# Float64 weights rebuilt with one VectorE instruction less, and a small add moved from VectorE to ScalarE, in an attention and expert kernel

## The chip, the cores and the metric

The kernel runs on one core of a Trainium2 chip. The metric is the device time of one execution in microseconds (us). The five engines are called by the profile's names: PE is TensorE (the matmuls; PEld its weight loads), DVE is VectorE, ACT is ScalarE, POOL is GpSimd, and SP issues DMAs.

## The reference

Three networks follow each other. Attention (4 batches, 8 heads, 512 local and 32 global tokens, head size 64) has a softmax whose sum gets 1e-9 added:

```python
def sm(s):
    s = s - np.max(s, axis=-1, keepdims=True)
    e = np.exp(s)
    return e / (np.sum(e, axis=-1, keepdims=True) + 1e-09)
```

Local tokens see 32 neighbours on either side and the global tokens; global tokens see all. Then a gated two-layer network follows, and a mixture of experts which sends each token to one of eight:

```python
xk = mu_k * x + (1.0 - mu_k) * x_prev
xr = mu_r * x + (1.0 - mu_r) * x_prev
k = np.maximum(xk @ w_k, 0.0)
v = k * k @ w_v
r = 1.0 / (1.0 + np.exp(-(xr @ w_r)))
return (r * v)
...
h = np.maximum(x[b, s] @ w1[e], 0.0)
out[b, s] = p[e] * (h @ w2[e])
```

The weights `w_k`, `w_r` and `w_v` of the middle network are multiplied by a float64 scalar when they are drawn, so they arrive as float64.

## The kernel before

`phase1` does the attention and the middle network, `Experts` the rest. `phase1` is a set of generators that a planner (`Sched`, lines 41 to 80) interleaves: each `yield op("D",.34)` names the engine of the instructions that follow and the duration which the planner assumes for them, with places in buffers that they need and free. The planner runs when the kernel is built. Its order is then sorted once more by the compiler's own model, and every engine works through its list in that fixed order.

`Attn` works on 16 units (a batch and a pair of heads); a unit has four items of 128 local tokens and one global item. `item` (line 195): PE makes the scores of two heads (L207); DVE adds the mask and takes the row's extreme (L213, two instructions); ACT takes the exponential with the sum beside it (L216, two); DVE adds 1e-9 to the two sums (L218, 128x2) and takes the reciprocal (L219); POOL multiplies (L222, two); PE transposes (L228); ACT and DVE copy the result out of PSUM; PE multiplies with the values (L236); ACT writes the result to `xT` (L240, L241). The probabilities lie in four buffers `pl`.

`Mix.weight` (line 386) brings one of 20 pieces of a float64 weight matrix (8 of `w_k`, 4 of `w_r`, 8 of `w_v`) into two float32 parts, a piece being 128x512 numbers. The high word of a float64 has an exponent field of 11 bits, of which the upper eight lie where a float32 has its exponent. The steps: ACT takes the absolute value of the high word, read as float32 (L403); DVE raises it to at least `LEAST` (L405), masks it and shifts it left by three (L407), puts in the sign and the upper exponent bit of the high word (L409) and three bits of the low word (L411); ACT rounds to the first part (L413); POOL subtracts to get the second (L415).

`Mix.mix` (line 430) blends each token with the one before it (POOL L441, DVE L444, ACT L446, POOL L448 into `xs`), and `Mix.run` multiplies (psk, psr, psv); these matmuls fill PE between the items of attention. When the last attention unit is done, `late` (line 726) frees the buffers of attention and loads the first expert weights into the tiles `st` (SP), which ACT (L778) and DVE (L781) split into two parts.

Of the kernel before, what the change touches and what calls it, by code (L numbers as in the profile page):

```python
# [10 lines left out]
F32=mybir.dt.float32; F32R=mybir.dt.float32r; BF=mybir.dt.bfloat16; I32=mybir.dt.int32  # L11
AF=mybir.ActivationFunctionType; ALU=mybir.AluOpType; X=mybir.AxisListType.X
# [1 line left out]
P=128; D=512; F=1024; E=8; SG=32; SL=512; S=544; NB=4; T=2176; HD=64; NK=9; NCH=17  # L14
NEG=-1e9
FRESH=-1.08674975e-07
LEAST=float(np.array(0x38000000,np.int32).view(np.float32))

def mm3(nc,out,wh,wl,xh,xl,first,last,order=None):

# [18 lines left out]
def op(e,d,need=(),free=(),when=None): return e,d,need,free,when  # L39
def wait(f): return "",0.0,(),(),f  # L40
# [42 lines left out]
class Attn:  # L83
# [111 lines left out]
    def item(s,u,i):  # L195


        nc=s.nc; b,pr=divmod(u,4); kw,qT=s.T[u]["k"],s.T[u]["q"]
        tag,n=("cm",3) if u<4 and i%2 else ("s",2)
        ks=slice(32*(i==0),224-32*(i==3)); w=1 if i in (1,2) else .87  # L200
        parts=s.parts(u)
        yield op("P",(.25+.13*len(parts) if len(parts)>1 else .8)*w,(tag,tag,"p"))
        S_=[s.ps.tile([P,512],F32,tag=tag,name="s_",bufs=n)[:,ks] for h in range(2)]
        for m,(x,y) in enumerate(parts):
            for h in range(2):
                r=slice(h*HD,(h+1)*HD)
                nc.tensor.matmul(S_[h],qT[r,x,i*P:(i+1)*P],kw[r,y,i,ks],start=m==0,stop=m==len(parts)-1)  # L207
        s.sdone[u]+=1
        p=s.pt_.pop(0)
        mx=s.sb.tile([P,8],F32,tag="mx",name="mx",bufs=5)  # L210
        yield op("D",.64*w,(),(tag,tag))
        for h in range(2):
            nc.vector.tensor_tensor_reduce(out=p[:,h,ks],in0=S_[h],in1=s.mask[:,ks],scale=-0.125,scalar=3e38,op0=ALU.add,op1=ALU.min,accum_out=mx[:,h:h+1])  # L213
        yield op("A",.93*w)
        for h in range(2):
            nc.scalar.activation(p[:,h,ks],p[:,h,ks],AF.Exp,bias=mx[:,h:h+1],scale=-1.0,accum_out=mx[:,4+h:5+h])  # L216
        yield op("D",.28)
        nc.vector.tensor_scalar(out=mx[:,4:6],in0=mx[:,4:6],scalar1=1e-9,scalar2=None,op0=ALU.add)  # L218
        nc.vector.reciprocal(mx[:,6:8],mx[:,4:6])  # L219
        yield op("G",.87*w)  # L220
        for h in range(2):
            nc.gpsimd.tensor_scalar(out=p[:,h,ks],in0=p[:,h,ks],scalar1=mx[:,6+h:7+h],scalar2=0.0,op0=ALU.mult,op1=ALU.add)  # L222
        yield op("P",.43,("pt","ph"),("p",),when=lambda: not s.early(u) or u in s.V)
        pt=s.ps.tile([P,2,2,P],F32,tag="pt",name="ptp",bufs=2)
        for c in range(2):

            for h in range(2):
                nc.tensor.transpose(pt[:,c,h],p[:,h,c*96:c*96+P],s.ident)  # L228
        s.pt_.append(p)
        P_=s.weights(u)  # L230
        yield from s.split(u,EV[i],P_,pt.rearrange("p c h q -> p c (h q)"),"pt",(.48,.61))
        yield op("P",.65 if len(parts)>1 else .87,("av",),("ph",),when=lambda: u in s.V)
        o=s.ps.tile([P,512],F32,tag="av",name="av",bufs=1)[:,:256]
        for c in range(2):
            for m,(x,y) in enumerate(parts):
                nc.tensor.matmul(o,s.v(u,x,i,c),P_[y][:,c],start=c==m==0,stop=c==1 and m==len(parts)-1)  # L236
        s.vdone[u]+=1
        yield op("A",.33,(),("av",))
        x=s.xT[b]; c0=1+SG+i*P
        nc.scalar.activation(x[0:64,pr,c0:c0+P],o[0:64,0:P],AF.Copy)  # L240
        nc.scalar.activation(x[64:128,pr,c0:c0+P],o[64:128,P:2*P],AF.Copy)  # L241
        yield wait(None)
        s.odone[u]+=1
# [3 lines left out]
    def v(s,u,w,i,c): return s.V[u][0][:,i,c] if s.early(u) else s.V[u][i//2][:,w,i%2,c]  # L247
# [83 lines left out]
class Mix:  # L331
# [54 lines left out]
    def weight(s,k,i):  # L386


        nc=s.nc; place="raw"+"v"*(k=="wv")
        yield op("Q",1.5,(place,))  # L390
        raws=s.raws[k=="wv"]; raw=raws.pop(0); raws.append(raw)
        v=lambda a: a[:,:,i*P:(i+1)*P] if k=="wk" else a[:,i:i+1]
        src=s.src[k].bitcast(I32).rearrange("(c p) (f t) -> p c f t",p=P,t=2)
        c=4 if k=="wk" else 1
        raw=raw.rearrange("p (c f t) -> p c f t",c=c,t=2); lo,hi=raw[:,:,:,0],raw[:,:,:,1]
        nc.sync.dma_start(raw.rearrange("p c f t -> p c (f t)"),v(src).rearrange("p c f t -> p c (f t)"))

        yield op("A",.52,("r",),when=lambda: k!="wv" or (s.may(S) and s.conv["wk"]==8 and s.conv["wr"]==4))
        if "wvh" not in s.W and k=="wv":
            for q,t in zip("hl",s.wplace()): s.W["wv"+q]=t.rearrange("p (c f) -> p c f",c=8)  # L400
        h,l=[v(s.W[k+x]) for x in "hl"]
        m=s.temp("w").rearrange("p (c f) -> p c f",c=c); a=m.bitcast(I32)
        nc.scalar.activation(m,hi.bitcast(F32),AF.Abs)  # L403
        yield op("D",.34)
        nc.vector.tensor_scalar(out=m,in0=m,scalar1=LEAST,scalar2=None,op0=ALU.max)  # L405
        yield op("D",.34)
        nc.vector.tensor_scalar(out=a,in0=a,scalar1=0x07FFFFFF,scalar2=3,op0=ALU.bitwise_and,op1=ALU.logical_shift_left)  # L407
        yield op("D",.6)
        nc.vector.scalar_tensor_tensor(out=a,in0=hi,scalar=-0x40000000,in1=a,op0=ALU.bitwise_and,op1=ALU.bitwise_or)  # L409
        yield op("D",.6,(),(place,))  # L410
        nc.vector.scalar_tensor_tensor(out=a,in0=lo,scalar=29,in1=a,op0=ALU.logical_shift_right,op1=ALU.bitwise_or)  # L411
        yield op("A",.52)
        nc.scalar.activation(h,m,AF.Copy)  # L413
        yield op("G",1.23,(),("r",))
        nc.gpsimd.tensor_sub(l,m,h.bitcast(F32))  # L415
        yield wait(None)
        s.conv[k]+=1
# [639 lines left out]
```

## Time and profile before

| what | us |
|---|---|
| median of 3 runs | 781.51 |
| lowest and highest run | 778.05, 782.53 |
| the profiled execution, its own time | 781.29 |
| its span in the trace | 779.6 |
| busy in the span: PE, DVE | 734.9, 509.7 |
| busy in the span: ACT, POOL | 396.5, 347.6 |

The span is what the profiler saw from the first to the last instruction; the time of the same execution is 1.7 us longer. Busy time is the time in which an engine had at least one instruction under way. An average over the span mixes stages: attention with the middle network runs to about 520 us, the experts after it.

### The profile page before, as it was taken

What the parts mean: (1) busy time and instruction counts of PE and PEld (TensorE: products, weight loads), DVE (VectorE), ACT (ScalarE), POOL (GpSimd) and SP (SyncE); (2) the same over time, 40 slices, a digit from 0 to 9 for tenths busy, and PEclk for the clock granted to TensorE, in tenths of its full rate; (3) what the DMA queues carried; (4) which work ended last, traced back from release to release, by engine and by line L of the source; (5) the groups of instructions that cost most, each with busy time, mean ns of one, the idle gap of its engine ahead of it and who ended that gap; (6) DMA issues with size and microseconds to landing.
All of it is one profiled execution on the core that took longest, in us unless ns stands there. A gap on an engine that the chain in (4) does not pass through costs nothing. (4 is left out here: it accounts for less than half of the span.)

```text
span 779.6 us, 14122 instructions
## 1 busy us (share of the span) xinstructions
PE 734.9 (94%) x4782; PEld 620.7 (80%) x4782; DVE 509.7 (65%) x1483; ACT 396.5 (51%) x985; POOL 347.6 (45%) x473
## 2 busy tenths in 40 slices
PE   6888888999999999999999899997999999999996
PEld 3655686888888888888888789775787999989884
DVE  6798878868487695696664875666764643617261
ACT  4796666665374664664663524233762622416151
POOL 6576756743537335545343342015553332514231
PEclk9998798999999999999999999999999999999998
DMA  6684123211211211212000500135875351705330
GB/s 156 156 226 126 58 76 106 57 51 36 65 31 27 64 40 37 65 32 78 12 13 28 175 32 12 57 107 215 284 266 209 122 178 39 271 30 182 123 98 17
DMA packets 93478, 77.04 MB, mean 99 GB/s; under 512 B 70462, under 2 KB 74558, under 8 KB 93378
## 3 DMA queue, kind: packets, MB, share of 16 engines
q1 hardware_dynamic: 89618, 64.27, 27.6%
q0 software_dynamic: 3760, 11.54, 4.1%
q8 instruction: 50, 0.82, 0.4%
q14 instruction: 50, 0.41, 0.2%
HBM read 66.87 MB, written 9.70 MB: 98 GB/s over the span
## 5 line engine op out<-in xcount | busy, mean ns | idle before, releaser
L222 POOL TENSOR_SCALAR pl<-pl,mx 128x192 f32<-128x192 f32 (+1 forms) x128 | 63.5, 508 | 86.8 <-DVE mx L219 41.6
L216 ACT ACTIVATE pl<-pl,mx 128x224 f32<-128x224 f32 (+1 forms) x128 | 58.8, 461 | 35.5 <-DVE mx L213 28.8
L21 PE MATMUL psk<-xs,slot0h 128*128 128x256 f32 x256 | 74.3, 296 | 0.8 <-ACT xs L446 0.8
L23 PE MATMUL psk<-xs,slot0h 128*128 128x256 f32 x256 | 73.6, 289 | 0.0
L24 PE MATMUL psk<-xs,slot0l 128*128 128x256 f32 x256 | 73.3, 288 | 0.0
L448 POOL TENSOR_TENSOR xs<-xm,xs 128x512 fp32r<-128x512 f32 (+1 forms) x36 | 46.3, 1298 | 40.9 <-ACT xs L446 40.9
L884 ACT ACTIVATE hh<-ph 128x256 fp32r<-128x256 f32 x56 | 21.6, 385 | 84.0 <-PE ph L24 82.8
L863 POOL DMA_INDIRECT xs<-y,idx x26 | 32.5, 1249 | 63.2 <-PE pt L870 39.2
L441 POOL TENSOR_SCALAR xm<-xT,mut 128x256 f32<-128x256 f32 (+7 forms) x96 | 42.7, 462 | 36.8 <-DVE xT L292 18.6
L932 POOL DMA_INDIRECT out_dram<-osb,idx x18 | 22.5, 1251 | 79.0 <-DVE osb L928 65.6
L21 PE MATMUL psv<-slot1h,kh 128*128 128x512 f32 x136 | 55.3, 407 | 0.0
L23 PE MATMUL psv<-slot1l,kh 128*128 128x512 f32 x136 | 54.3, 400 | 0.0
L24 PE MATMUL psv<-slot1h,kl 128*128 128x512 f32 x136 | 54.2, 398 | 0.0
L21 PEld LDWEIGHTS psk<-xs,slot0h 128*128 128x128 f32 x256 | 48.7, 193 | 1.8 <-ACT xs L446 0.9
L23 PEld LDWEIGHTS psk<-xs,slot0h 128*128 128x128 f32 x256 | 48.8, 191 | 1.2
L228 PE MATMUL ptp<-ident,pl 128*128 128x128 f32 x256 | 43.7, 291 | 6.1 <-DVE kw L119 1.3
L24 PEld LDWEIGHTS psk<-xs,slot0l 128*128 128x128 f32 x256 | 48.9, 191 | 0.6
L236 PE MATMUL av<-ph,v 128*128 128x256 f32 x192 | 45.0, 295 | 2.3 <-DVE xT L292 1.9
L885 DVE SCALAR_TENSOR_TENSOR hl<-ph,hh 128x256 fp32r<-128x256 f32 x56 | 23.7, 422 | 33.0 <-ACT hh L884 32.7
L444 DVE SCALAR_TENSOR_TENSOR xm<-xT,mut,xm 128x256 f32<-128x256 f32 (+7 forms) x96 | 41.3, 463 | 3.1 <-POOL xm L441 3.0
L119 DVE TENSOR_TENSOR plo<-ptp,ph 128x512 fp32r<-128x512 f32 x48 | 32.7, 684 | 14.9 <-ACT ph L117 14.7
L228 PEld LDWEIGHTS ptp<-ident,pl 128*128 128x128 f32 x256 | 30.4, 147 | 13.0 <-issue 3.1
(732 smaller groups left out, 2458.9 us busy)
## 6 DMA issues: line engine op xcount, KB each, us to landing
st<-in_moe_w_dram SPq DMA_DIRECT2D x42, 512.0 KB, 4.3
sw<-in_moe_w_dram SPq DMA_DIRECT2D x22, 512.0 KB, 4.3
y<-r SPq DMA_DIRECT2D x17, 256.0 KB, 2.1
qn<-in_q_l_dram SPq DMA_DIRECT2D x32, 128.0 KB, 2.9
kn<-in_k_l_dram SPq DMA_DIRECT2D x32, 128.0 KB, 3.0
earlyh<-in_moe_w_k_dram SPq DMA_DIRECT2D x8, 512.0 KB, 4.9
raw<-in_moe_w_v_dram SPq DMA_DIRECT2D x8, 512.0 KB, 3.8
vn<-in_v_l_dram SPq DMA_DIRECT2D x24, 96.0 KB, 2.1
```

The lines of the kernel that those rows point to most:

```text
L21: i=nc.tensor.matmul(out,wh,xh,start=first,stop=False)
L23: nc.tensor.matmul(out,wh,xl,start=False,stop=False)
L24: return nc.tensor.matmul(out,wl,xh,start=False,stop=last)
L119: nc.vector.tensor_sub(out[1],x,out[0].bitcast(F32))
L216: nc.scalar.activation(p[:,h,ks],p[:,h,ks],AF.Exp,bias=mx[:,h:h+1],scale=-1.0,accum_out=mx[:,4+h:5+h])
L222: nc.gpsimd.tensor_scalar(out=p[:,h,ks],in0=p[:,h,ks],scalar1=mx[:,6+h:7+h],scalar2=0.0,op0=ALU.mult,op1=ALU.add)
L228: nc.tensor.transpose(pt[:,c,h],p[:,h,c*96:c*96+P],s.ident)
L236: nc.tensor.matmul(o,s.v(u,x,i,c),P_[y][:,c],start=c==m==0,stop=c==1 and m==len(parts)-1)
L441: nc.gpsimd.tensor_scalar(out=x[:,u,o:o+k],in0=s.xT[b][:,c,q:q+k],scalar1=m[:,1,c:c+1],scalar2=0.0,op0=ALU.mult,op1=ALU.add)
L444: nc.vector.scalar_tensor_tensor(out=x[:,u,o:o+k],in0=s.xT[b][:,c,1+q:1+q+k],scalar=m[:,0,c:c+1],in1=x[:,u,o:o+k],op0=ALU.mult,op1=ALU.add)
L448: nc.gpsimd.tensor_sub(xl[:,cs,:n],x[:,:,:n],xh[:,cs,:n].bitcast(F32))
L863: s.nc.gpsimd.indirect_dma_start(out=s.xs[i][:,j,:],out_offset=None,in_=s.y,in_offset=IndirectOffsetOnAxis(ap=s.idx[:,ch:ch+1],axis=0))
```

## The change

The absolute value on ACT (L403) becomes a copy with a scale of 2 to the -112. That lowers the float32 exponent by 112, which is 896 in the 11-bit field; a magnitude that is too small becomes zero there, so the raising to `LEAST` on DVE is gone. The sign is kept through the scaling, so the mask has one bit more and the later step takes the sign alone from the high word. In `item` the addition of 1e-9 moves from DVE to ACT, as a copy with a bias on a 128x2 tile, in the same group as the exponentials; the planner's durations follow. Behind line 406 all numbers of the changed kernel are two lower: its L405 is the mask and shift that was L407, its L407 and L409 are the steps that were L409 and L411, its L411 is the rounding that was L413.

```diff
--- before.py
+++ after.py
@@ -14,7 +14,7 @@
 P=128; D=512; F=1024; E=8; SG=32; SL=512; S=544; NB=4; T=2176; HD=64; NK=9; NCH=17
 NEG=-1e9
 FRESH=-1.08674975e-07
-LEAST=float(np.array(0x38000000,np.int32).view(np.float32))
+REBIAS=2.0**-112
 
 def mm3(nc,out,wh,wl,xh,xl,first,last,order=None):
 
@@ -211,11 +211,11 @@
         yield op("D",.64*w,(),(tag,tag))
         for h in range(2):
             nc.vector.tensor_tensor_reduce(out=p[:,h,ks],in0=S_[h],in1=s.mask[:,ks],scale=-0.125,scalar=3e38,op0=ALU.add,op1=ALU.min,accum_out=mx[:,h:h+1])
-        yield op("A",.93*w)
+        yield op("A",.2+.93*w)
         for h in range(2):
             nc.scalar.activation(p[:,h,ks],p[:,h,ks],AF.Exp,bias=mx[:,h:h+1],scale=-1.0,accum_out=mx[:,4+h:5+h])
-        yield op("D",.28)
-        nc.vector.tensor_scalar(out=mx[:,4:6],in0=mx[:,4:6],scalar1=1e-9,scalar2=None,op0=ALU.add)
+        nc.scalar.activation(mx[:,4:6],mx[:,4:6],AF.Copy,bias=1e-9)
+        yield op("D",.15)
         nc.vector.reciprocal(mx[:,6:8],mx[:,4:6])
         yield op("G",.87*w)
         for h in range(2):
@@ -400,13 +400,11 @@
             for q,t in zip("hl",s.wplace()): s.W["wv"+q]=t.rearrange("p (c f) -> p c f",c=8)
         h,l=[v(s.W[k+x]) for x in "hl"]
         m=s.temp("w").rearrange("p (c f) -> p c f",c=c); a=m.bitcast(I32)
-        nc.scalar.activation(m,hi.bitcast(F32),AF.Abs)
+        nc.scalar.activation(m,hi.bitcast(F32),AF.Copy,scale=REBIAS)
         yield op("D",.34)
-        nc.vector.tensor_scalar(out=m,in0=m,scalar1=LEAST,scalar2=None,op0=ALU.max)
-        yield op("D",.34)
-        nc.vector.tensor_scalar(out=a,in0=a,scalar1=0x07FFFFFF,scalar2=3,op0=ALU.bitwise_and,op1=ALU.logical_shift_left)
+        nc.vector.tensor_scalar(out=a,in0=a,scalar1=0x0FFFFFFF,scalar2=3,op0=ALU.bitwise_and,op1=ALU.logical_shift_left)
         yield op("D",.6)
-        nc.vector.scalar_tensor_tensor(out=a,in0=hi,scalar=-0x40000000,in1=a,op0=ALU.bitwise_and,op1=ALU.bitwise_or)
+        nc.vector.scalar_tensor_tensor(out=a,in0=hi,scalar=-0x80000000,in1=a,op0=ALU.bitwise_and,op1=ALU.bitwise_or)
         yield op("D",.6,(),(place,))
         nc.vector.scalar_tensor_tensor(out=a,in0=lo,scalar=29,in1=a,op0=ALU.logical_shift_right,op1=ALU.bitwise_or)
         yield op("A",.52)
```

The planner's times are different, so the whole order of `phase1` is. Three places follow, each as built, before and then with the change.

The list of VectorE near its start, where the first pieces of `w_k` (`w`, `earlyh`) stand between the mask additions (`pl`, `mx`) of the first items. Before:

```order
L405 TENSOR_SCALAR w<-w 128x512
L407 TENSOR_SCALAR w<-w 128x512
L213 ISA pl_112,mx<-s__270,mask 128x192
L213 ISA mx 128x1
L409 SCALAR_TENSOR_TENSOR w<-earlyh,w 128x512
L405 TENSOR_SCALAR w<-w 128x512
L213 ISA pl_112,mx<-s__271,mask 128x192
L213 ISA mx 128x1
L411 SCALAR_TENSOR_TENSOR w<-earlyh,w 128x512
L407 TENSOR_SCALAR w<-w 128x512
L213 ISA pl_113,mx<-s__280,mask 128x224
L213 ISA mx 128x1
```

With the change:

```order
L405 TENSOR_SCALAR w<-w 128x512
L407 SCALAR_TENSOR_TENSOR w<-earlyh,w 128x512
L213 ISA pl_112,mx<-s__218,mask 128x192
L213 ISA mx 128x1
L409 SCALAR_TENSOR_TENSOR w<-earlyh,w 128x512
L405 TENSOR_SCALAR w<-w 128x512
L213 ISA pl_112,mx<-s__219,mask 128x192
L213 ISA mx 128x1
L213 ISA pl_113,mx<-s__225,mask 128x224
L213 ISA mx 128x1
L407 SCALAR_TENSOR_TENSOR w<-earlyh,w 128x512
L213 ISA pl_113,mx<-s__226,mask 128x224
```

The L405 of before is gone, and the steps of a piece stand closer together; no addition L218 is left on this engine.

The list of ScalarE over the same items (`slot0h` is the first part of `w_k`, rounded). Before:

```order
L216 ACTIVATE pl_112,mx<-pl_112,mx 128x192
L403 ACTIVATE w<-earlyh 128x512
L216 ACTIVATE pl_112,mx<-pl_112,mx 128x192
L413 ACTIVATE slot0h<-w 128x4x128
L216 ACTIVATE pl_113,mx<-pl_113,mx 128x224 x2
L216 ACTIVATE pl_114,mx<-pl_114,mx 128x224
L111 ACTIVATE earlyl<-ptq 128x4x128
L216 ACTIVATE pl_115,mx<-pl_115,mx 128x192
L413 ACTIVATE slot0h<-w 128x4x128
```

With the change:

```order
L216 ACTIVATE pl_112,mx<-pl_112,mx 128x192
L411 ACTIVATE slot0h<-w 128x4x128
L403 ACTIVATE w<-earlyh 128x512
L216 ACTIVATE pl_112,mx<-pl_112,mx 128x192
L216 ACTIVATE pl_113,mx<-pl_113,mx 128x224
L217 ACTIVATE mx<-mx 128x2
L216 ACTIVATE pl_113,mx<-pl_113,mx 128x224
L217 ACTIVATE mx<-mx 128x2
L411 ACTIVATE slot0h<-w 128x4x128
```

An addition L217 stands behind the exponentials of its item, here one row behind or with another item's exponential between. In the whole list there are 64, between one and four rows behind the second exponential of their item; the first 27 stand 2.15 rows behind it on the mean, so that 1.15 rows lie between.

The list of ScalarE where attention ends and the first expert weights come in (`og` is the last global item, `xs` the blended tokens, `st` the loaded weights, `slot2h` their first part). Before:

```order
L285 ACTIVATE og<-avg,mxg 64x128
L558 ACTIVATE lt<-psl 10x128
L446 ACTIVATE xs<-xm 128x512
L778 ACTIVATE slot2h<-st_5851 128x1024
L446 ACTIVATE xs<-xm 128x512
L603 ACTIVATE ex,sums<-L,nmx 128x8 x2
L778 ACTIVATE slot2h<-st_5852 128x1024
L778 ACTIVATE slot2h<-st_5853 128x1024
```

With the change:

```order
L285 ACTIVATE og<-avg,mxg 64x128
L556 ACTIVATE lt<-psl 10x128
L776 ACTIVATE slot2h<-st_5814 128x1024
L444 ACTIVATE xs<-xm 128x512
L601 ACTIVATE ex,sums<-L,nmx 128x8 x2
L444 ACTIVATE xs<-xm 128x512
L776 ACTIVATE slot2h<-st_5815 128x1024
L776 ACTIVATE slot2h<-st_5816 128x1024
```

Before, the first of the two blends L446 stands ahead of the first split L778; with the change both blends (L444 there) stand behind the first split (L776 there).

## Rows read from the trace of the kernel before

**Rows 1.** The page: busy totals of all engines, then VectorE (DVE) in 40 slices of 19.5 us.

```profile
PE 734.9 (94%) x4782; PEld 620.7 (80%) x4782; DVE 509.7 (65%) x1483; ACT 396.5 (51%) x985; POOL 347.6 (45%) x473
...
DVE  6798878868487695696664875666764643617261
```

**Rows 2.** Windows, all engines: start:end, length, busy us (instructions) each, PEclk, DMA share, GB/s.

```profile
14.00:145.00 131.00, 113.29 (x630) 85.06 (x630) 109.98 (x324) 91.99 (x271) 86.35 (x113) 0.90 0.44 118
145.00:380.00 235.00, 234.29 (x1768) 201.86 (x1767) 168.77 (x611) 134.41 (x395) 114.28 (x193) 1.00 0.18 46
...
430.00:442.00 12.00, 8.97 (x73) 8.07 (x73) 10.90 (x37) 7.16 (x15) 4.08 (x4) 0.86 0.49 175
```

**Rows 3.** Windows, all engines: two shorter stretches of the first stage.

```profile
14.00:20.00 6.00, 5.23 (x15) 2.25 (x14) 6.00 (x22) 3.81 (x14) 4.56 (x6) 1.00 0.44 61
44.00:68.00 24.00, 18.91 (x95) 12.42 (x95) 23.78 (x67) 19.68 (x57) 16.80 (x18) 0.93 0.81 220
```

**Rows 4.** Waits of TensorE (PE), 14 to 160 us: releaser, us in total, times, longest.

```profile
PE av L236 <- DVE xT L292: 1.4, 1, 1.4
PE ptp L228 <- DVE kw L119: 1.3, 1, 1.3
PE s__1065 L207 <- DVE mx L213: 1.3, 1, 1.3
```

**Rows 5.** Groups of VectorE instructions, 14 to 145 us: shape xcount | busy, mean ns | idle.

```profile
L405 DVE TENSOR_SCALAR w<-w 128x512 f32<-128x512 f32 x17 | 11.6, 681 | 0.4 <-ACT w L403 0.3
...
L407 DVE TENSOR_SCALAR w<-w 128x512 int32<-128x512 int32 x18 | 8.8, 488 | 0.1
L218 DVE TENSOR_SCALAR mx<-mx 128x2 f32<-128x2 f32 x27 | 8.7, 325 | 4.2 <-ACT pl L216 4.1
```

**Rows 6.** Windows of single VectorE lines: L405 in one stretch, then L218 in two.

```profile
44.00:68.00 24.00, 4.64 (x6) 0.93 0.81 220
...
14.00:20.00 6.00, 1.59 (x2) 1.00 0.44 61
44.00:68.00 24.00, 1.42 (x4) 0.93 0.81 220
```

**Rows 7.** Timeline of VectorE, then one row of GpSimd (POOL), 43 to 51 us: start, us.

```profile
43.52 0.41 DVE L405 TENSOR_SCALAR w<-w 128x512 f32<-128x512 f32 x1
43.85 0.68 DVE L411 SCALAR_TENSOR_TENSOR w<-earlyh,w 128x512 int32<-128x512 int32 x1
...
48.49 0.15 DVE L218 TENSOR_SCALAR mx<-mx 128x2 f32<-128x2 f32 x1
48.55 0.48 DVE L114 COPY ph<-ptg 128x320 f32<-128x320 f32 x1
...
49.88 1.16 DVE L405 TENSOR_SCALAR w<-w 128x512 f32<-128x512 f32 x1
...
49.44 1.31 POOL L415 TENSOR_TENSOR slot0l<-w,slot0h 128x512 fp32r<-128x512 f32 x1 [0.59 <-ACT slot0h L413]
```

**Rows 8.** Groups of ScalarE (ACT) instructions, whole run: shape xcount | busy, mean ns | idle.

```profile
L403 ACT ACTIVATE w<-earlyh 128x512 f32<-128x512 f32 x12 | 8.1, 672 | 3.6 <-DMA earlyh<-in_moe_w_k_dram 3.3 <-DMA earlyh<-in_moe_w_r_dram 0.3
...
L603 ACT ACTIVATE ex<-L,nmx 128x8 f32<-128x8 f32 x17 | 4.9, 291 | 1.4 <-DVE nmx L589 1.4
```

**Rows 9.** Timeline of ScalarE, then GpSimd, then TensorE, 434 to 438 us.

```profile
434.92 0.63 ACT L446 ACTIVATE xs<-xm 128x512 fp32r<-128x512 f32 x1 [0.41 <-DVE xm L444]
436.42 1.06 ACT L778 ACTIVATE slot2h<-st 128x1024 fp32r<-128x1024 f32 x1 [0.87 <-DMA st<-in_moe_w_dram]
437.38 0.61 ACT L446 ACTIVATE xs<-xm 128x512 fp32r<-128x512 f32 x1
...
435.63 1.27 POOL L448 TENSOR_TENSOR xs<-xm,xs 128x512 fp32r<-128x512 f32 x1 [0.92 <-ACT xs L446]
...
435.60 0.62 PE L21 MATMUL psk<-xs,slot0h 128*128 128x256 f32 x3 [0.81 <-ACT xs L446]
...
437.75 0.56 PE L23 MATMUL psk<-xs,slot0h 128*128 128x256 f32 x1
```

## The prediction

> **What bounds the kernel now.** I read the busy totals first, then the windows, then the waits of TensorE, and last single lines. The totals name TensorE: 734.9 us busy of a span of 779.6 [rows 1]. What a change on VectorE and ScalarE can give lies in TensorE's gaps and in its lower clock, so the question is where those are. The windows answer it [rows 2]. From 145 to 380 us TensorE is busy for 234.3 of 235 us at full clock: whatever VectorE saves there is hidden behind matmuls. From 14 to 145 us it is busy for only 113.3 of 131 us, and the granted clock is 0.90 on the mean. So 17.7 us are idle, and about 113.3 x 0.10 = 11.3 us more go to the lower of its two clock levels. That stage is where the change can pay. The slices show VectorE at its fullest in it [rows 1], and the shorter windows show two stretches where VectorE has no gap left: 6.00 of 6 us from 14 to 20, 23.8 of 24 us from 44 to 68, while ScalarE has over four us free in the second [rows 3]. There VectorE sets the pace. In the rest of the stage it is busy for 110.0 - 29.8 = 80.2 of 101 us, and TensorE waits for it only now and then: three waits that VectorE ended there make 4.0 us [rows 4].
>
> **The conversion of the weights.** Per piece one 128x512 instruction leaves VectorE, L405; 17 of the 20 lie in the stage, 11.6 us by their durations [rows 5]. What an absent one gives back has two ends. The next instruction starts 0.33 us after an undisturbed one (43.52 to 43.85), the least; the most is its whole duration, 0.68 us on the mean, which contains waits [rows 5, 7]. ScalarE's scaled copy takes the place of the absolute value on the same tile; I count no difference, between nothing and 0.1 us for each of 20 at 0.67 us [rows 8], and ScalarE has the room.
>
> **The addition of 1e-9.** 64 additions leave VectorE, 27 of them in the stage, 8.7 us by their durations [rows 5]. The ends again: the next instruction starts 0.06 us after an undisturbed one [rows 7], and the mean duration is 0.325. On ScalarE no such instruction exists in the trace. The nearest is the exponential of a 128x8 tile, 0.291 us [rows 8]; the bounds are nothing and twice that row, because the addition waits for the sum of its own engine. I take 0.29, the row itself: 27 x 0.29 = 7.8 us more, so ScalarE goes from 92.0 to 99.8 of 131 us [rows 2]. In the full stretch it has 19.7 of 24 us and gets four or five of them, 1.4 us. It stays below VectorE, so I count nothing on the path. The other 37 lie beside matmuls that leave TensorE no gap; were that cover gone, they would cost at most 37 x 0.29 = 10.7 us.
>
> **What of it lies on the path.** In the two full stretches are six L405 and six L218: 4.64 + 1.59 + 1.42 = 7.65 us by duration [rows 6], and 6 x 0.33 + 6 x 0.06 = 2.3 us by the distance of starts. Between them lie the waits. One is seen in the rows: L405 at 49.88 takes 1.16 us and ends shortly after a GpSimd instruction that ran from 49.44 for 1.31 us [rows 7]. When the instruction is gone, its wait is either gone too or passes to the next one on VectorE. The rows favour neither end, so I take the middle, 5.0 us. In the rest of the stage 6.9 + 5.7 = 12.6 us leave 80.2 us of work, 16%; applied to the 4.0 us of waits that gives 0.6 us. The clock I leave as it is: it is 1.00 where TensorE has no gap (145 to 380 us) and 0.93 in the full stretch with its 5.1 us of gaps [rows 2, 3], and no row says how many gaps must go before it holds. Its bounds are 0 and the 11.3 us above.
>
> The Trainium skill ("SBUF — State Buffer", section "SBUF: two separate sides") says that VectorE and GpSimd lock a shared pair of ports against each other for a whole instruction, and that a VectorE instruction with two SBUF inputs takes part as well. By that rule the two-input steps of the conversion, which stay, inherit the wait; the sum would then go by the lower end, 2.3 us instead of 5.0. The wait in rows 7 agrees with the lock.
>
> **Where attention ends.** The order is made anew, and at one place I can price it. Before, ScalarE's first blend L446 starts at 434.92, ahead of the first split L778, which had to wait for a DMA and starts at 436.42; the blend behind that split starts at 437.38 [rows 9]. With the change the first blend stands behind the split: 2.46 us later. GpSimd's second part follows 0.08 us after the blend and takes 1.27, so it would end at 437.38 + 0.63 + 0.08 + 1.27 = 439.36, and TensorE's matmul that started at 437.75 would start at about 439.4. I count +1.7 us, between 0 (the DMA comes sooner) and +2.5 (all of the delay). SP's loads are reordered too, expert weights excepted; I count nothing; a load that comes late would cost about as much as that DMA wait, 0.87 us [rows 9], and this stays in the range.
>
> **Sum.** -5.0 - 0.6 + 1.7 = -3.9 us against the profiled execution's 781.29 (span 779.6; the execution lies 0.2 us below the median 781.51): **777.4 us**. With the ends above the forecast's own range is 773.0 (-7.65 - 0.6) to 781.5 (-2.3 + 2.5).
>
> **The rivals.**
> *The wait passes on.* If the next VectorE instruction inherits each wait for GpSimd, the relief is 2.3 us, and outside the full stretches 11 x 0.33 + 21 x 0.06 = 4.9 us, 6% of 4.0, or 0.2. With +1.7 that is 780.5, no change that a measurement of this kernel can tell (that takes about 0.5%, 3.9 us). For it: the rows of the conversion stand closer together than before, on the same ports, and L407, which stays, has waits of its own (0.488 us on the mean [rows 5]). Against it: a later instruction often finds GpSimd idle, as GpSimd is busy for 86 of 131 us [rows 2].
>
> *A larger gain.* Gaps and the lower clock stand together in the rows, and matmuls at the lower clock make the items late. If half of the gaps (8.9 us) and half of the clock's loss (5.7 us) come back, the sum is -8.9 - 5.7 + 1.7 = -12.9, or 768.4. For it: VectorE is the busiest helper in the whole stage [rows 2]. Against it: outside the full stretches the rows name VectorE for only 4.0 us of TensorE's waits [rows 4].
>
> *Slower: the addition waits in ScalarE's list.* The 27 additions of the stage stand behind 1.15 other rows on the mean. At 0.67 us a row [rows 8], with ScalarE busy for 92 of 131 us, a row takes 0.67 / 0.70 = 0.96 us, so the reciprocal comes 1.1 us later. Four buffers `pl` are in turn, so a delay of 1.1 us for 27 items makes 27 / 4 x 1.1 = 7.4 us. With the small relief (2.3 + 0.2) and +1.7 this is 787.9. It decides, against the forecast's -3.9, from a delay of 3.9 x 4 / 27 = 0.58 us per item. For it: the order itself. Against it: before, the same addition stood in the list of an engine that was fuller still.
>
> **Chances.** Forecast 0.47, wait passes on 0.23, larger gain 0.13, slower 0.17. The limit for faster is 777.6: the forecast's range lies a little more below it than above, so 0.27 of it go to faster and 0.20 to the same; the larger gain goes to faster, and 0.02 of the passing wait. Of the slower rival 0.15 stay slower. That gives faster 0.42, same 0.43, slower 0.15. The range 770 to 786 leaves out the far halves of the outer two cases, about 0.17.
>
> **What would show it.** In the new profile: VectorE below 95 of 131 us in 14 to 145; no full stretch of 24 us there; 64 additions on ScalarE of about 0.3 us; the last item of unit 8 earlier by about 5 us; the first blend near the end of attention behind the first split and 1 to 2.5 us of new TensorE idle there. If VectorE's remaining conversion steps are longer than before (L407 was 0.488), the wait passed on. If GpSimd's multiplications wait longer for the reciprocal, the slower rival is right. The forecast is wrong if the stage to 145 us is not shorter although VectorE has gaps.

## The result: slower by 1.4%, and the profile after

| | median, us | lowest to highest, runs |
|---|---|---|
| before | 782.80 | 778.05 to 785.27, 6 |
| with the change | 793.47 | 791.35 to 795.40, 6 |

The ratio is 1.0139 with a 95% interval of 1.0106 to 1.0173. The forecast was 777.4 us, its range 770 to 786. The profiled execution of the changed kernel took 791.35 us, its span is 789.6.

The page of the changed kernel, busy totals and VectorE's slices (before: [rows 1]):

```profile
PE 739.8 (94%) x4782; PEld 624.1 (79%) x4782; DVE 492.2 (62%) x1399; ACT 408.1 (52%) x1049; POOL 347.7 (44%) x473
...
DVE  6588588667584686585674784567665553627261
```

VectorE has 84 instructions and 17.5 us less, ScalarE 64 instructions and 11.6 us more, as the change says. TensorE has the same 4782 matmuls, and they keep it busy for 4.9 us longer. The windows of the changed kernel (before: [rows 2, 3]):

```profile
14.00:145.00 131.00, 113.29 (x653) 85.76 (x654) 97.06 (x278) 96.70 (x294) 87.18 (x115) 0.92 0.44 118
145.00:380.00 235.00, 229.79 (x1663) 196.09 (x1661) 157.75 (x560) 132.95 (x406) 111.52 (x187) 0.99 0.18 45
14.00:20.00 6.00, 4.68 (x15) 2.60 (x15) 5.98 (x23) 4.68 (x17) 3.58 (x6) 1.00 0.43 60
44.00:68.00 24.00, 17.98 (x85) 11.88 (x85) 21.69 (x59) 21.66 (x69) 18.41 (x20) 0.87 0.79 227
```

The full stretch of 24 us is gone (21.69 in place of 23.78); that from 14 to 20 us is as full as before (5.98 of 6). VectorE is 12.9 us less busy in 14 to 145 us, and TensorE is busy for exactly as long there as before. The surprise is the second row: in 145 to 380 us, where TensorE had no gap, 5.2 us of 235 are idle now and the granted clock is 0.99.

To see where the 10 us came in, the two spans are cut at points where the same work is done: the last transpose of unit 4 (the lists hold the same numbers of psk, psr, psv, av and score matmuls ahead of it in both orders), that of unit 16 (the same), and the last matmul of psy, behind which only experts follow. The windows between these points, before:

```profile
0.00:96.73 96.73, 78.06 (x377) 54.15 (x377) 76.85 (x245) 65.97 (x197) 64.81 (x113) 0.91 0.55 145
96.73:432.29 335.56, 327.15 (x2420) 281.38 (x2420) 242.00 (x841) 192.70 (x558) 165.12 (x268) 0.98 0.18 47
432.29:516.82 84.53, 81.11 (x508) 69.11 (x509) 55.95 (x171) 33.05 (x65) 26.51 (x32) 0.98 0.24 85
516.82:779.60 262.78, 248.61 (x1478) 216.10 (x1478) 134.91 (x229) 104.76 (x166) 91.16 (x60) 0.98 0.44 152
```

and with the change:

```profile
0.00:96.21 96.21, 75.74 (x376) 53.78 (x376) 65.50 (x208) 68.11 (x212) 62.20 (x113) 0.93 0.55 146
96.21:439.60 343.39, 333.25 (x2420) 284.16 (x2419) 234.35 (x789) 202.18 (x607) 169.00 (x269) 0.98 0.18 46
439.60:527.12 87.52, 82.28 (x511) 69.88 (x511) 57.38 (x175) 33.17 (x65) 25.40 (x32) 0.96 0.23 82
527.12:789.60 262.48, 248.48 (x1478) 216.32 (x1478) 134.92 (x229) 104.69 (x166) 91.13 (x60) 0.99 0.45 152
```

The front gained 0.5 us, the middle (units 5 to 16) lost 7.8, the hand-over lost 3.0, the experts are as before. In the middle the 2420 matmuls (single records can be missing) keep TensorE busy for 6.1 us longer, and 1.7 us more are idle.

The groups of VectorE in 14 to 145 us with the change (before: [rows 5]), then the addition on ScalarE, whole run:

```profile
L405 DVE TENSOR_SCALAR w<-w 128x512 int32<-128x512 int32 x18 | 10.7, 593 | 4.4 <-ACT w L403 4.4
L407 DVE SCALAR_TENSOR_TENSOR w<-earlyh,w 128x512 int32<-128x512 int32 x11 | 10.7, 970 | 0.1
...
L219 DVE RECIPROCAL mx<-mx 128x2 f32<-128x2 f32 x24 | 3.8, 158 | 3.5 <-ACT mx L217 3.4
...
L217 ACT ACTIVATE mx<-mx 128x2 f32<-128x2 f32 x64 | 12.6, 198 | 0.9
```

Before, the mask and shift took 0.488 us on the mean [rows 5], and the step behind it is this group:

```profile
L409 DVE SCALAR_TENSOR_TENSOR w<-earlyh,w 128x512 int32<-128x512 int32 x11 | 7.7, 704 | 0.0
```

So the mask and shift went from 0.488 to 0.593 us, and the next step from 0.704 to 0.970: part of the waits did pass on to the steps that stay. Not every group got longer: the same next step on the pieces of `w_v` (8 of them, input `raw`) went from 1.124 to 0.987. The three steps that stay together are busy for 45.4 us in 14 to 145 us, 41.1 before, so about 4 of the 11.6 us of L405 came back in them. VectorE also waits 4.4 us for the scaled copy L403 now.

### The profile page after: what moved, and what is told of

It reads as the page before. It is cut to its first block, busy times and chain, and to the rows that moved or that the text cites. A ratio compares the mean times of both kernels' runs of the same rounds, so it can differ in the third digit from the quotient of the medians.

```text
span 789.6 us, 14015 instructions
## 1 busy us (share of the span) xinstructions
PE 739.8 (94%) x4782; PEld 624.1 (79%) x4782; DVE 492.2 (62%) x1399; ACT 408.1 (52%) x1049; POOL 347.7 (44%) x473
## 5 line engine op out<-in xcount | busy, mean ns | idle before, releaser
L21 PE MATMUL psk<-xs,slot0h 128*128 128x256 f32 x256 | 75.4, 301 | 3.5 <-ACT xs L444 3.5
L23 PE MATMUL psk<-xs,slot0h 128*128 128x256 f32 x256 | 75.0, 294 | 0.0
L446 POOL TENSOR_TENSOR xs<-xm,xs 128x512 fp32r<-128x512 f32 (+1 forms) x36 | 45.7, 1278 | 40.1 <-ACT xs L444 32.9
L23 PE MATMUL psv<-slot1l,kh 128*128 128x512 f32 x136 | 55.6, 409 | 2.9 <-POOL slot1l L413 2.9
L21 PEld LDWEIGHTS psk<-xs,slot0h 128*128 128x128 f32 x256 | 49.4, 196 | 5.0 <-ACT xs L444 4.0
L23 PEld LDWEIGHTS psk<-xs,slot0h 128*128 128x128 f32 x256 | 49.9, 195 | 1.1 <-issue 0.2
L228 PE MATMUL ptp<-ident,pl 128*128 128x128 f32 x256 | 45.4, 295 | 3.1 <-DVE g L385 0.8
```

Of the source, the lines that this page charges most:

```text
L21: i=nc.tensor.matmul(out,wh,xh,start=first,stop=False)
L23: nc.tensor.matmul(out,wh,xl,start=False,stop=False)
L446: nc.gpsimd.tensor_sub(xl[:,cs,:n],x[:,:,:n],xh[:,cs,:n].bitcast(F32))
```

## The experiments

Fifteen kernels ran, each beside the kernel before; each does the whole computation. In the kernels called pinned, a table of the instructions of each engine keeps the planner and the compiler's model from choosing the order of `phase1` (shortened; `ORDER` holds the table):

```diff
     sched.run()
+    keep_order(tc,ORDER)
     return m
...
+def keep_order(tc,text):
...
+    L={}
+    for i in tc.nc.cur_bb.bb.instructions: L.setdefault(str(i.engine).split(".")[-1],[]).append(i)
+    for e,o in tables.items():
+        for a,b in zip(o,o[1:]):
+            tc.add_manual_dep(L[e][b],L[e][a].name,mybir.DependencyInfo(mybir.DependencyClass.NoSync,mybir.DependencyReason.SCHED_ONLY))
```

### Instructions and order apart: four pinned kernels

**The change's instructions in the order of before** (ORDER is the order of before without L405, each addition directly behind its item's second exponential).

> The changed instructions in exactly the order of before on all five engines (TensorE, GpSimd and SP row for row; the removed rows gone, each addition directly behind the second exponential of its item on ScalarE). Theory A, the new order costs the time: 778 to 783 us, at most 0.5% from before, and a little faster if VectorE's relief reaches TensorE at all (my prediction's term was -5.6 us, that is 776). Theory B, the instructions cost it (the addition delays the reciprocal on ScalarE, the scaled copy is slower): 790 to 795 us, like the change.

Measured: 778.38 us, ratio 0.9929 (0.9904 to 0.9954).

**The instructions of before in the change's order** (the reverse: the absent instructions are put directly ahead of the steps that they stood ahead of).

> The instructions of before in the order of the change on TensorE, GpSimd and SP row for row; the clamp stands directly ahead of its mask and the addition directly ahead of its reciprocal on VectorE. Theory A: 790 to 800 us, as slow as the change or slower, since VectorE keeps its 84 instructions. Theory B: 778 to 784 us, like before.

Measured: 809.93 us, ratio 1.0332 (1.0307 to 1.0357). Theory A had the way right, but its range ended at 800 us.

**The weights' part alone, and the addition alone, in the order of before** (the first two kernels' edit, one half of the change's diff each).

> Only the weights' part (scaled copy, no clamp) in the order of before; the addition stays on VectorE. Theory A: 776 to 782 us, -0 to -5 us against before, as much as the relief of VectorE by 20 instructions in the first stage gives. Theory B with the copy as its cost: over 786 us; with the addition as its cost: like before.

Measured: 776.46 us, ratio 0.9914 (0.9888 to 0.9940).

> Only the addition moved to ScalarE, in the order of before; the clamp stays. Theory A: 779 to 784 us, within 0.5% of before (0.19 us each on ScalarE in the profile of the change, 27 in the first stage). Theory B with the addition as its cost: over 786 us.

Measured: 783.55 us, ratio 1.0006 (0.9983 to 1.0029).

What follows: the change's instructions are faster by 0.7%, and all of that is the weights' part; the moved addition gives nothing. The new order costs 2.1% under the new instructions (0.9929 to 1.0139) and 3.3% under the old ones, so it suits a lighter VectorE, as it was made for one, but it loses with both. The middle and the hand-over of the first of these kernels stand near those of before:

```profile
0.00:93.25 93.25, 75.86 (x376) 52.88 (x377) 69.09 (x211) 69.68 (x217) 62.91 (x113) 0.93 0.57 151
93.25:430.13 336.88, 327.73 (x2421) 281.53 (x2420) 231.72 (x791) 200.79 (x602) 165.50 (x269) 0.98 0.18 47
430.13:515.77 85.64, 82.55 (x508) 70.47 (x508) 55.45 (x171) 33.16 (x65) 26.53 (x32) 0.96 0.24 84
```

Against the changed kernel it is 6.5 us shorter in the middle and 1.9 us at the hand-over. These two profiled executions lie 10.5 us apart, the medians 15.1 us: the one is the slowest of its kernel's six, the other the fastest. The middle goes with the order: in the profiles of all five kernels with the order of before on TensorE (one of them joins six items, see below) it takes 335.6 to 336.9 us, in the changed kernel and the four that repair places of its order 343.4 to 345.4, and with the instructions of before in the changed order 348.9. The changed kernel's loss is its order.

### Three places of the new order, repaired one by one

**The hand-over.** In the changed kernel ScalarE's first split L776 waits for its weights, and the first blend L444 behind it (before: [rows 9]). TensorE's rows there, then ScalarE's:

```profile
443.81 0.37 PE L592 MATMUL psr<-ident,fe 128*1 128x128 f32 x1 [1.12 <-DVE fe L586]
445.95 1.01 PE L21 MATMUL psk<-xs,slot0h 128*128 128x256 f32 x3 [1.76 <-ACT xs L444]
447.84 0.37 PE L592 MATMUL psr<-ident,fe 128*1 128x128 f32 x1 [0.88 <-DVE fe L586]
...
444.32 1.06 ACT L776 ACTIVATE slot2h<-st 128x1024 fp32r<-128x1024 f32 x1 [3.30 <-DMA st<-in_moe_w_dram]
445.28 0.61 ACT L444 ACTIVATE xs<-xm 128x512 fp32r<-128x512 f32 x1
```

The repair, as lists of the engines and not as code:

```diff
 ScalarE
+L444 xs<-xm
 L776 slot2h<-st
-L444 xs<-xm
 VectorE
+L586 fe<-fe,base,fr
 L779 slot2l<-st,slot2h
-L586 fe<-fe,base,fr
```

> The changed kernel in its own order, with two pairs of instructions exchanged where attention ends: ScalarE's first blend L444 stands ahead of the first split L776 again, and VectorE's second step of fe (L586) ahead of the first L779. The changed kernel has 793.5 us. Theory A (the order at this place costs what the trace shows): from the transpose avt of the last unit to the second matmul psk on the new tokens it takes 439.60 to 447.86, 8.26 us, before 432.29 to 437.75, 5.46 us; the difference of 2.8 us comes back, 790.7 us, and TensorE's wait of 1.76 us for the blend is gone. Theory B (the loads of the expert weights set the end of this place, whichever engine waits for them first): the wait returns a few us later, 793.5 us as before the exchange.

Measured: 790.98 us, ratio 1.0143 (1.0088 to 1.0197). The place itself got shorter: from the last avt (438.58) to the second row of psk, L23 at 444.70, it takes 6.1 us in place of 8.3 (439.60 to 447.86). Not all of it came back: a gap of 2.15 us stands a step earlier now, where it was 1.12, because L586 is held beside a GpSimd instruction. TensorE, VectorE and GpSimd in the repaired kernel:

```profile
443.82 0.37 PE L592 MATMUL psr<-ident,fe 128*1 128x128 f32 x1 [2.15 <-DVE fe L586]
...
442.52 1.37 DVE L586 SCALAR_TENSOR_TENSOR fe<-fe,base,fr 128x1 f32<-128x1 f32 x2
...
442.49 1.26 POOL L446 TENSOR_TENSOR xs<-xm,xs 128x512 fp32r<-128x512 f32 x1 [0.92 <-ACT xs L444]
```

The 2.1 us at this place are below what six runs with this scatter (789.74 to 800.25 us) can show, so the gain of this repair stays unclear.

**Near 325 us.** VectorE, then GpSimd, then TensorE in the changed kernel:

```profile
325.63 1.17 DVE L581 SCALAR_TENSOR_TENSOR fr<-L,first 128x2 f32<-128x2 f32 x1
326.72 0.34 DVE L213 CUSTOM_DVE_ANT_0 pl<-s__4432,mask 128x192 f32<-128x192 f32 x1
...
324.29 2.49 POOL L192 TENSOR_TENSOR v<-vn,v 128x512 fp32r<-128x512 f32 x2
...
327.13 0.37 PE L207 MATMUL s__4472<-kw,qT 64*128 64x224 f32 x1 [1.58 <-DVE mx L213]
```

A 128x2 instruction lasts 1.17 us and ends at 326.80, GpSimd's at 326.78. The window behind it shows TensorE at the lower of its two levels throughout:

```profile
328.00:334.00 6.00, 6.00 (x26) 4.66 (x26) 3.39 (x19) 4.36 (x20) 3.84 (x6) 0.50 0.27 61
```

```diff
 VectorE
+L213 pl,mx<-s__4432,mask
+L213 pl,mx<-s__4433,mask
 L580 mx<-L
 L581 fr<-L,first
-L213 pl,mx<-s__4432,mask
 L582 m<-L,mx
-L213 pl,mx<-s__4433,mask
```

> The changed kernel in its own order, with five instructions of VectorE in another order near 325 us: the two mask additions L213 of the first item of unit 13 come ahead of L580, L581 and L582 of the router. In the changed kernel L581, a 128x2 instruction, lasts 1.17 us from 325.63 beside a GpSimd instruction with two SBUF inputs (324.29 for 2.49 us), the mask additions wait behind it, TensorE idles 1.58 us and then runs at half clock from 328 to about 335 us, 3.4 us lost. Theory A (the wait behind L581 starts it, and the clock follows the gap): the gap shrinks to about 0.5 us, the clock holds, 1.1 + 3.4 = 4.5 us come back, 789.0 us. Theory A, smaller: the gap shrinks but the clock falls all the same, 792.4 us. Theory B (the mask additions are held beside GpSimd just as L581 is): nothing comes back, 793.5 us, and L213 lasts over 1 us there.

Measured: 793.88 us, ratio 1.0139 (1.0097 to 1.0181). VectorE and TensorE there:

```profile
332.50 0.36 DVE L213 CUSTOM_DVE_ANT_0 pl<-s__4432,mask 128x192 f32<-128x192 f32 x1
...
333.14 0.59 DVE L581 SCALAR_TENSOR_TENSOR fr<-L,first 128x2 f32<-128x2 f32 x1
...
332.92 0.49 PE L207 MATMUL s__4472<-kw,qT 64*128 64x224 f32 x2 [0.45 <-DVE mx L213]
...
334.59 0.27 PE L592 MATMUL psr<-ident,fe 128*1 128x128 f32 x1 [0.80 <-DVE fe L586]
```

The mask additions are not held (0.36 us), and the gap fell from 1.58 to 0.45 us; but `fe`, which is later now, opens one of 0.80 us, and the clock falls all the same:

```profile
334.00:340.00 6.00, 5.37 (x24) 4.44 (x24) 3.81 (x24) 4.36 (x18) 4.36 (x8) 0.66 0.30 67
```

**Both.**

> Both exchanges together, in the changed kernel's own order otherwise. Theory A (these two places are a large part of what the new order costs, and independent of each other): 2.8 + 4.5 = 7.3 us, 786.2 us, so about half of the 15 us between the changed kernel and the same instructions in the order of before (778.4) lies in two places. Theory B (the loss is spread over the whole attention stage): above 791 us.

Measured: 795.08 us, ratio 1.0161 (1.0106 to 1.0215). Theory B: these places are not half of the loss.

**The heads of an item.** The scores of an item's two heads lie on different halves of TensorE's rows (64 partitions each). In the middle stage the new order has 24 blocks in which one head's three matmuls stand alone, before it was 12. Counted until the next matmul starts, one head alone takes 0.52 us, both together 0.53. That the two halves work side by side is what the Trainium skill says ("TensorEngine Tiling (Array Packing)", section "Key Properties": different tiles can run matmuls in parallel); the trace agrees. One head alone, in the changed kernel:

```profile
238.56 0.59 PE L207 MATMUL s__3103<-kw,qT 64*128 64x224 f32 x3
239.08 0.39 PE L236 MATMUL av<-plo,v 128*128 128x256 f32 x1
```

All L207 in the middle, before and with the change, by busy time (columns: TensorE, its weight loads; the expectation below counts from start to start, the difference is the same 4.8 us):

```profile
96.73:432.29 335.56, 30.85 (x264) 21.74 (x264) 0.98 0.18 47
```

```profile
96.21:439.60 343.39, 35.64 (x264) 25.44 (x264) 0.98 0.18 46
```

```diff
 TensorE (15 items)
-L207 s__3103 x3
 L236 av x5
-L207 s__3104 x3
+L207 s__3103, s__3104 in turn, three each
```

> The changed kernel in its own order, except that on TensorE the three score matmuls (L207) of one head and those of the other stand side by side for 15 items of units 5 to 16, where the new order had put 1 to 20 other matmuls between them. In the traces the three matmuls of one head alone take 0.52 us and those of both heads together 0.53 us, so an item whose heads are apart costs 0.5 us more; in the middle stage the order of before has 12 such lone blocks and the new one 24, and L207 takes 26.7 us there before and 31.5 us with the change. Theory A (part of what the new order costs is that heads run one after the other): 15 times 0.5 us, up to 7.5 us come back, 786 us. Theory B (the other matmuls between the heads only hid a wait for VectorE, which now shows, as each item's first mask addition starts later): nothing, 793 us or more.

Measured: 793.71 us, ratio 1.0138 (1.0105 to 1.0171). L207 in the middle, all instructions of the middle, and then the longest waits of TensorE in it:

```profile
99.37:444.73 345.36, 28.53 (x264) 20.25 (x264) 0.97 0.18 46
...
99.37:444.73 345.36, 329.45 (x2419) 281.24 (x2419) 229.50 (x789) 201.65 (x607) 169.08 (x269) 0.97 0.18 46
```

```profile
PE psv L23 <- POOL slot1l L413: 3.4, 1, 3.4
PE s__3838 L207 <- DVE mx L213: 2.3, 1, 2.3
PE s__4472 L207 <- DVE mx L213: 1.6, 1, 1.6
PE psk L21 <- DVE row L596: 1.3, 1, 1.3
```

The scores take 7.1 us less, and the stage is no shorter: TensorE is idle for 15.9 us of it, 10.1 with the change. The waits for VectorE's `mx` and `row` of 2.3 and 1.3 us are new, those for `slot1l` and `s__4472` were there without the edit (2.9 and 1.6). So Theory B: what stood between the heads had covered waits. They are 5.8 of the 7.1 us. All of TensorE's busy time fell by only 3.8 us, so the other matmuls took 3.3 us more, and the granted clock is 0.97 in place of 0.98; 0.01 of 345 us is 3.5 us, an estimate that fits. The same edit for six items in the better kernel:

> The weights' part of the change alone in the order of before (776.5 us), with the six items of units 5 to 16 whose heads stood apart in that order joined on TensorE, too (1 to 5 matmuls lay between). Theory A (a lone block costs 0.5 us): 6 times 0.5 is 3 us, 773.5 us, faster than every kernel so far. Theory B (what lay between hid a wait): 776.5 us or more.

Measured: 776.91 us, ratio 0.9921 (0.9889 to 0.9952), no different from 776.46.

### Is it this order, or any order made anew?

Six kernels are not pinned, so the planner and the compiler's model make their order. Their instructions are those of before, of the change or of its weights' half, and their edits these (shortened; those that name the change are against it):

```diff
 new_code_old_numbers (the change's instructions)
-        yield op("A",.2+.93*w)
+        yield op("A",.93*w)
-        yield op("D",.15)
+        yield op("D",.28)
+        yield op("D",.34)
 weights_planned_anew: the weights' half of the change alone
 one_planner_number (the instructions of before)
-        yield op("D",.28)
+        yield op("D",.30)
 change_extra_0, change_extra_01
-        yield op("A",.2+.93*w)
+        yield op("A",.93*w)     and .1+.93*w
 change_recip_028
-        yield op("D",.15)
+        yield op("D",.28)
```

> The change's instructions, but the planner keeps the durations that it had before (two steps of 0.34 for the conversion, 0.93 for the exponentials, 0.28 for the reciprocal); nothing is pinned, so the compiler's model sorts the list anew. The order is nearer to that of before: 1442 of TensorE's rows differ from it, against 4195 with the change. Theory A (the planner's new numbers made the bad order): between 776 and 783 us. Theory B (whatever disturbs the order of before loses, as that order was the one found good): over 787 us.

> The weights' part of the change alone, nothing pinned: the planner drops one step of 0.34 us per piece and makes its order anew, 1105 of TensorE's rows stand elsewhere than before. Theory A (the gain of the weights' part is real, and a small move of the order costs little): 775 to 780 us. Theory B (any order made anew costs over 0.5%): 783 us or more.

> The kernel before with all its instructions, and one number of the planner changed: the duration that it assumes for the addition of 1e-9 with the reciprocal is 0.30 in place of 0.28 us. Nothing is pinned; 3579 of TensorE's rows stand elsewhere, and the middle stage has 26 lone blocks of scores (before 12). Theory A (a new order costs time by itself, whatever the instructions): slower than before by over 0.5%, about 788 to 800 us. Theory B (only the numbers of this change make a bad order): 783 us, as before.

> The change with one number of the planner taken back: 0.93 us for the exponentials in place of 0.2 + 0.93, so the planner thinks the moved addition free on ScalarE. 2849 of TensorE's rows stand elsewhere than in the changed kernel. Theory A (this number makes the bad order): back to 776 to 781 us. Theory B (a draw; no number by itself decides): anywhere between 776 and 802 us, not ordered by the size of the number.

> The change with half of that number, 0.1 + 0.93 us, near what the trace shows the addition to hold ScalarE for (0.10 us until the next instruction starts). 2572 of TensorE's rows stand elsewhere than in the changed kernel. Theory A (the number 0.2 is the cause, in proportion): about 786 us, between the changed kernel and the run with 0. Theory B (a draw): not between the two.

> The change with the planner's other new number taken back: 0.28 us for the reciprocal in place of 0.15. 2155 of TensorE's rows stand elsewhere than in the changed kernel. Theory A (the 0.2 is the cause): 793 us, as the changed kernel. Rival (the 0.15 is the cause): 776 to 781 us. Theory B (a draw): anywhere between 776 and 802 us.

| kernel | ratio, interval | middle of the profiled execution, us |
|---|---|---|
| new_code_old_numbers | 0.9974 (0.9947 to 1.0002) | 333.4 |
| weights_planned_anew | 0.9974 (0.9946 to 1.0002) | 337.4 |
| change_recip_028 | 1.0035 (1.0014 to 1.0056) | 340.4 |
| the change | 1.0139 (1.0106 to 1.0173) | 343.4 |
| change_extra_0 | 1.0167 (1.0131 to 1.0203) | 347.7 |
| change_extra_01 | 1.0181 (1.0147 to 1.0215) | 351.8 |
| one_planner_number | 1.0214 (1.0170 to 1.0258) | 348.7 |

One number changed by 0.02 us, with every instruction as before, costs 2.1%. Half of the change's 0.2 us is no better than all of it or nothing, so that number by itself is not the cause; taking the reciprocal's number back helps by 1.0%, but no reason for it is shown. That looks like a draw: of these seven orders none beats the kernel before beyond its interval. But a rival stands. By the counts in the expectations, the orders of weights_planned_anew and new_code_old_numbers are near to that of before (1105 and 1442 of TensorE's rows elsewhere), and they lose 0.6 and 0.5% against the same instructions in it; those of one_planner_number and the change are far from it (3579 and 4195) and lose 2.1% each. So it may be that the order of before is a good one, and that moving far from it costs; no run tells the two apart. The front is not what sets them apart in their profiles, one execution each: weights_planned_anew and four of the five with the change's instructions reach unit 4 at 89.1 to 93.9 us, the kernel before at 96.7. The middle stage all but sets the rank. For the kernel with the change of 0.02 us it reads

```profile
98.06:446.72 348.66, 338.41 (x2431) 286.67 (x2432) 248.85 (x843) 196.01 (x559) 169.13 (x269) 0.98 0.18 46
```

so TensorE is busy for 11.3 us longer than before (327.15), for all but the same matmuls.

The fastest kernel of all is the weights' part alone in the order of before, 776.46 us; it beats the kernel before and the change (with six items joined it is the same, 776.91).

## Why the prediction was wrong, by its steps

- **The sum of the instructions** was right in total: -5.0 and -0.6 us were forecast, and in the order of before the change gives -0.7%, 5.6 us. That is partly luck. Of the 7.65 us in the full stretches 4.64 are the weights' and 1.59 + 1.42 = 3.01 the addition's, so that the 5.0 us mean 3.0 for the one and 2.0 for the other; measured alone, the weights give 0.9%, 6.7 us, and the addition nothing (1.0006). In the profile of the weights' part alone the gain lies in the front, where the forecast had it: unit 4 is reached at 92.26 us in place of 96.73, and the middle takes 335.62 in place of 335.56. One execution can't prove that (see the end).
- **"I count nothing on the path" for ScalarE**: an addition takes 0.198 us in place of the assumed 0.29, and there are 64. That none of it lies on the path is not shown: alone in the order of before it frees VectorE of 64 instructions and gains nothing, so something takes the relief back.
- **The hand-over** (+1.7 us, between 0 and 2.5) was the right mechanism, a little small: blend behind split behind a DMA, 1.76 us of idle at psk where it was 0.81 [rows 9], 2.8 us more from the last avt to the second row of psk, 3.0 us for the stage.
- **The step that failed** is the rest of the order: "where attention ends: the order is made anew, and at one place I can price it", with everything else at nothing, and "from 145 to 380 us ... whatever VectorE saves there is hidden behind matmuls". The second sentence speaks of VectorE's savings and says nothing of what a new order takes: a stage in which TensorE has almost no gap can still lose. The middle lost 7.8 us, 6.1 of them as busy time for the same matmuls and 1.7 as idle time; the new order as a whole costs 2.1%, and in the order of before the same instructions gain 0.7%. The forecast had no term for that, and its range ended at 786. L207 makes 4.8 of the 6.1 us, but that is where the time shows and not its cause: without these blocks the stage is as long.
- **The rivals.** *The wait passes on* was partly right: two of the steps that stay got longer by 0.1 and 0.27 us, all of them together by 4.3 us, and VectorE's 97.06 of 131 us missed the forecast's "below 95". *A larger gain* needed TensorE's gaps in the front to close; they did not (17.7 us idle in 14 to 145 us, before and with the change). *Slower* had the right sign (it gave 787.9 us), and what was named for it did appear: GpSimd's multiplications wait longer for the reciprocal in 14 to 145 us. The wait with the change:

```profile
POOL pl L222 <- DVE mx L219: 19.1, 11, 5.4
```

  and the same before:

```profile
POOL pl L222 <- DVE mx L219: 6.8, 6, 2.4
```

  But it is not what costs the time: with the addition alone in the order of before this wait is 16.2 us, and the kernel is as fast as before (1.0006). It may be why the addition gives nothing.
- **The signs named.** Unit 8 was to end 5 us earlier: with the change it ends 2.4 us later (204.9 for 202.5), in the order of before 3.8 us earlier (198.7). The forecast's mechanism exists, and the order undoes it.

What stays open: which choices of the new order cost the middle its 7.8 us, and why. Three places that the trace named, two of them in the middle, were repaired, and each time other waits or the lower clock took their place; whether a repair of all of them at once would bring it back was not tried.

## What to carry to other kernels

Where a planner makes the order from assumed durations, an edit of a few instructions is two changes, and the second can be the larger: run the new instructions in the old order first, then let the order be made anew, and keep whichever is faster. The forecast of such an edit needs a term for the order (here, against the same instructions in the order of before, +0.5% to +2.5% over seven orders), and a stage that is full of matmuls is not safe from it. A gap that one exchange closes says little while the next dependent step is as late: look for what would be late next before counting the gap as gain.

## What the runs showed that was not expected

The front stage of one and the same order differs from run to run. Up to unit 4 the kernels blend_first and masks_first have the list of the changed kernel, and in their profiled executions it took 94.3 and 102.6 us:

```profile
0.00:94.33 94.33, 76.17 (x377) 53.97 (x377) 65.97 (x208) 67.95 (x212) 61.97 (x113) 0.93 0.56 149
```

```profile
0.00:102.61 102.61, 79.14 (x376) 55.52 (x376) 68.07 (x208) 68.37 (x212) 61.65 (x113) 0.87 0.52 137
```

The granted clock is 0.93 in one and 0.87 in the other, and TensorE is idle for 18.2 and 23.5 us. So a single profile can't show a gain of 5 us there; the stage behind it repeats to 1.5 us (343.4 to 344.9 us in four executions of nearly the same list).

A VectorE instruction of 128x2 and a pair of 128x1, with two SBUF inputs each, took over a microsecond (1.17 and 1.37 us) beside GpSimd instructions that read SBUF, and ended within 0.15 us of them (L581 at 326.80 and 326.78, L586 at 443.89 and 443.75). The Trainium skill ("SBUF — State Buffer", section "SBUF: two separate sides") says that such a pair excludes each other for a whole instruction; the trace agrees. With GpSimd idle, the same instruction of the changed kernel took 0.15 us:

```profile
168.78 0.15 DVE L581 SCALAR_TENSOR_TENSOR fr<-L,first 128x2 f32<-128x2 f32 x1
```
